# A mixer block on one core: weights and late x tiles moved to the second DMA ring, w1 loaded in three parts, and a new order of tiles

## The chip, the cores and the metric

The kernel runs on one core of a Trainium2 chip. TensorE does the matrix multiplications; DVE (VectorE), ScalarE and GpSimd do the other arithmetic; SyncE only issues transfers (DMAs). A "ring" is the queue of transfers that one engine, here SyncE or ScalarE, has issued. A transfer "lands" when the last of its data is reported. The "granted clock" is TensorE's clock as a share of full speed. The metric is the device time in microseconds, the median of several executions; the profile is of one execution. Its "span" (first to last instruction) is some 1.3 us shorter than the time. Ratios are the mean time of one kernel's fast runs over that of the other's of the same rounds, so not quite the ratio of the medians quoted.

## The reference

```python
B, S, D, F = 1, 2048, 512, 1792                      # bf16
h  = gelu(layernorm(x) @ w1)
hs = concat(h[:, :, 0:128]   shifted by +1 token, h[:, :, 128:256] by -1,
            h[:, :, 256:384] by +2,               h[:, :, 384:512] by -2) @ w2
x1 = x + hs
return x1 + gelu(layernorm(x1) @ w3) @ w4
```

2048 tokens are 16 tiles of 128. For each tile: statistics, norm, a transpose, the projection by w1 ("up1"), the mix by w2, a second norm and transpose ("tile 16 + t"), the up projection by w3 ("up2", in groups of tiles) and the down projection by w4.

## The kernel before

All instructions are recorded with their dependences and put in order by a list scheduler; what is tuned are the tables below. `SCRIPT` is TensorE's order. `ty:n` transposes tile n on TensorE (four matmuls against the identity and a copy by ScalarE or DVE); a tile without `ty` is transposed by a DMA issued from SyncE. `LOADS` is the order in which loads are issued; `@act` puts one on the ScalarE ring instead of SyncE's.

```python
GROUPS = {1: (1, 1, 1, 1, 2, 1, 4, 2, 2, 1), 2: (2, 4, 4, 2, 4)}
LOADS = """
x1 x2 tp2 x0@act w1a w1b x3 x4-5 tp5 w2a w2b x6-7 w3 tp17 w4a x8-10 w4b tp6 x11-12 tp1 tp16 x13-15
"""
SCRIPT = """
warm:9 sa:0 sb:0 ty:1 ra:0 rb:0 ty:2 up1:1 th:0 up1:2 mix:0 ty:3 ty:5 mix:1 ty:4 up1:3-4 ty:16 mix:2 ty:17
mix:3 up2:0 mix:4 up1:5 down:1 down:0 mix:5 up1:6-7 ...
"""
# ... the transpose of a tile that TensorE does not transpose
if q not in pe_tp:
    pg.add("sp", f"tp{q}",
           lambda e: e.dma_start(xT[:, :, P * t : P * (t + 1)], xn_buf[:, slot(q), :], transpose=True),
           reads=[(("xn", slot(q), hh), q) for hh in (0, 1)],
           writes=[(("xT", t, c), layer) for c in range(DC)], queue="tp")
# ... idle-filling matmuls at the start, on zeros
def f(e):
    for _ in range(n):
        ins = e.matmul(o_ps[:, b, :], zeros[:], rows, start=True, stop=True)
    return ins
```

In a load's name, w1a and w1b are halves of w1, `w1r` and `w1s` its last two quarters, x4-5 two tiles of x. The first tile runs as rows: `ra:0` and `rb:0` are two matmuls each over the first and second half of w1.

## Time and profile before

| | before |
|---|---|
| time | 135.79 us (135.78 to 136.6, 3 runs) |
| TensorE busy | 130.9 of 134.6 us, granted clock 1.00 |
| second row pair of tile 0 starts | 6.65 us |
| from there to the last matmul's end | 126.2 us |
| tile 6's DMA transpose | issued 15.96, landed 21.86, wanted 23.8 us |

The table is read from the chain of waits and from the records of the DMA engines, which give each packet's start and each landing. For what follows it matters that the first transpose by DMA is wanted only after all weights have landed (the last at 21.4 us). The lines stand in the prediction.

### The profile page before, as it was taken

The numbers are of one execution on the slowest core, as the hardware profiler recorded it, in microseconds if no ns is written. First come the engines' busy times: TensorE is split into PE (matmuls) and PEld (weight loads), VectorE is DVE, ScalarE is ACT, GpSimd is POOL, SyncE is SP. The second block draws the span as 40 slices with busy tenths as digits, with TensorE's granted clock in tenths as the row PEclk, the third lists the DMA queues.
The fourth block names the chain that finished last, engine by engine and source line by source line (L and its number), as shares of the span: only waits on it lengthen the run. The fifth ranks groups of instructions, "written<-read, shape, count | busy, mean of one in ns | idle before, by whom it ended". The sixth has DMA issues, their size and how long they took to land.

```text
span 134.6 us, 2001 instructions
## 1 busy us (share of the span) xinstructions
PE 130.9 (97%) x776; PEld 71.5 (53%) x789; DVE 50.8 (38%) x134; ACT 58.4 (43%) x92; POOL 29.7 (22%) x68
## 2 busy tenths in 40 slices
PE   8799999999999999999999999999999999999994
PEld 3287688544656444478544444444444444444464
DVE  2689996856178930070061004232222200012222
ACT  5779349989544275547315554000000155520000
POOL 2444549892102860006010001200000000000000
DMA  5999998445452134100411000211111100001112
GB/s 136 323 345 399 361 304 234 90 81 105 90 115 85 24 75 98 39 0 0 83 39 39 0 0 0 65 52 44 39 39 53 64 0 0 0 5 39 39 39 78
DMA packets 21289, 12.19 MB, mean 91 GB/s; under 512 B 13856, under 2 KB 20768, under 8 KB 21280
## 3 DMA queue, kind: packets, MB, share of 16 engines
q1 hardware_dynamic: 20704, 11.80, 32.7%
q10 hardware_dynamic: 576, 0.26, 0.7%
q8 instruction: 6, 0.10, 0.3%
q14 instruction: 3, 0.02, 0.1%
HBM read 6.82 MB, written 2.10 MB: 66 GB/s over the span
## 4 chain that ended last, share of the span: by engine, by line
PE 93%; DMA 4%; SPq 1%; issue 1%; DVE 0%
PE y_ps L626 46%; PE o_ps L695 36%; PE o_ps L666 10%; DMA w_sb<-in_w_dram 4%; PE y_ps L490 1%; SPq L368 1%; PE y_ps L528 0%; SPq L377 0%; DVE o_sb L703 0%; PE o_ps L594 0%; SPq L857 0%
## 5 line engine op out<-in xcount | busy, mean ns | idle before, releaser
L626 PE MATMUL y_ps<-xnT,w_sb 128*128 128x512 bf16 (+2 forms) x421 | 63.4, 308 | 0.2
L626 PEld LDWEIGHTS y_ps<-xnT,w_sb 128*128 128x128 bf16 x424 | 38.3, 98 | 24.8
L641 ACT ACTIVATE h2T<-y_ps 128x1024 bf16<-128x1024 f32 (+1 forms) x29 | 28.6, 993 | 48.8 <-PE y_ps L626 48.6
L695 PE MATMUL o_ps<-w_sb,h2T 128*128 128x512 bf16 (+3 forms) x247 | 48.6, 355 | 0.3
L695 PEld LDWEIGHTS o_ps<-w_sb,h2T 128*128 128x128 bf16 x252 | 23.5, 98 | 24.7
L703 DVE TENSOR_TENSOR o_sb<-o_ps,x_sb 128x512 bf16<-128x512 f32 (+3 forms) x18 | 11.4, 632 | 47.1 <-PE o_ps L695 47.1
L423 POOL TENSOR_TENSOR rstd<-mv,neghalf 128x1 f32<-128x1 f32 x21 | 11.5, 549 | 23.6 <-DVE mv L418 14.8
L416 DVE BATCH_NORM_STATS2 st<-x_sb 128x6 f32<-128x512 bf16 x21 | 14.1, 678 | 3.4 <-DMA x_sb<-in_x_dram 3.2
L666 PE MATMUL o_ps<-w_sb,hT 128*128 128x512 bf16 x59 | 14.9, 379 | 0.3
L423 POOL TENSOR_TENSOR rstd<-vpe,neghalf 128x1 f32<-128x1 f32 x11 | 6.0, 547 | 29.4 <-DVE vpe L412 29.3
L673 DVE SCALAR_TENSOR_TENSOR x_sb<-o_ps,x_sb 128x512 bf16<-128x512 f32 x5 | 3.4, 686 | 19.2 <-PE o_ps L666 19.2
L641 ACT ACTIVATE hT<-y_ps 128x512 bf16<-128x512 f32 (+1 forms) x10 | 8.1, 807 | 5.5 <-PE y_ps L626 5.3
L677 DVE TENSOR_TENSOR x_sb<-o_ps,x_sb 128x512 bf16<-128x512 f32 x11 | 7.6, 687 | 4.4 <-PE o_ps L666 4.1
L666 PEld LDWEIGHTS o_ps<-w_sb,hT 128*128 128x128 bf16 x64 | 6.0, 98 | 5.7
L457 POOL TENSOR_SCALAR xn_buf<-x_sb,rstd,nmr 128x512 bf16<-128x512 bf16 x11 | 8.4, 765 | 0.8 <-DVE nmr L450 0.4
L400 ACT ACTIVATE junk<-x_sb 128x512 bf16<-128x512 bf16 x11 | 6.9, 624 | 2.2 <-DVE x_sb L673 2.2
L454 ACT ACTIVATE xn_buf<-x_sb,nmr,rstd 128x512 bf16<-128x512 bf16 x8 | 6.3, 806 | 0.6 <-POOL nmr L450 0.6
L445 DVE TENSOR_SCALAR xn_buf<-x_sb,mv,rstd 128x512 bf16<-128x512 bf16 x12 | 5.3, 442 | 2.8 <-POOL rstd L423 2.6
L720 PE MATMUL o_ps<-zeros 128*128 128x512 bf16 x9 | 4.0, 631 | 0.4 <-DVE zeros L347 0.4
L395 ACT ACTIVATE junk<-x_sb 128x512 bf16<-128x512 bf16 x6 | 3.7, 624 | 0.8 <-DMA x_sb<-in_x_dram 0.8
L418 DVE BATCH_NORM_AGGREGATE mv<-st 128x2 f32<-128x9 f32 x21 | 3.8, 189 | 0.3
L450 POOL TENSOR_SCALAR nmr<-mv,rstd 128x1 f32<-128x1 f32 x13 | 3.4, 263 | 0.7
(34 smaller groups left out, 28.6 us busy)
## 6 DMA issues: line engine op xcount, KB each, us to landing
out_dram<-o_sb SPq DMA_DIRECT2D x15, 128.0 KB, 1.7
w_sb<-in_w_dram SPq DMA_DIRECT2D x1, 1792.0 KB, 9.7
w_sb<-in_w_dram SPq DMA_DIRECT2D x2, 896.0 KB, 11.5
w_sb<-in_w_dram SPq DMA_DIRECT2D x4, 256.0 KB, 5.2
x_sb<-in_x_dram SPq DMA_DIRECT2D x3, 256.0 KB, 5.1
x_sb<-in_x_dram SPq DMA_DIRECT2D x2, 384.0 KB, 8.9
x_sb<-in_x_dram SPq DMA_DIRECT2D x3, 128.0 KB, 2.6
xnT<-xn_buf SPq DMA_TRANSPOSE x24, 2.5
```

The lines of the kernel that those rows point to most:

```text
L400: (lambda d: (lambda e: e.activation(d, src, ACT_F.Square, accum_out=sums[:, q, 1:2])))(junk[:, b, :]),
L416: pg.add("dve", f"bnst{q}", lambda e: e.bn_stats(st9[:, q, 0:6], src), reads=rs, writes=[(("st", q), 0)], dur=605)
L423: lambda e: e.tensor_tensor(col(rstd), var, neghalf[:], ALU.pow),
L445: lambda e: e.tensor_scalar(dst, src, mv[:, q, 0:1], rstd[:, q : q + 1], ALU.subtract, ALU.mult),
L454: f = lambda e: e.activation(dst, src, ACT_F.Identity, bias=nmr[:, q : q + 1], scale=rstd[:, q : q + 1])
L457: f = lambda e: e.tensor_scalar(dst, src, rstd[:, q : q + 1], nmr[:, q : q + 1], ALU.mult, ALU.add)
L626: ins = e.matmul(y_ps[:, p, W * i : W * (i + 1)], wsb[:, dc, P * fc : P * (fc + 1)], src[:, dc, P * t0 : P * t0 + W], start=(dc == 0), sto ...
L641: (lambda d, s: (lambda e: e.activation(d, s, ACT_F.Gelu_apprx_tanh)))(dst, ysrc),
L666: ins = e.matmul(dst, hT[:, j, c0 : c0 + P], w2_sb[:, j, :], start=(j == 0), stop=(j == DC - 1))
L677: f = lambda e: e.tensor_tensor(x1_sb[:, t, :], dst, x_sb[:, t, :], ALU.add)
L695: ins = e.matmul(dst, h2T[:, fc, P * t : P * (t + 1)], w4_sb[:, fc, cs], start=(fc == 0), stop=(fc == FC - 1))
L703: (lambda d, c: (lambda e: e.tensor_tensor(o_sb[:, oi, c], d, x1_sb[:, t, c], ALU.add)))(dst, cs),
```

## The change

Intent: let SyncE's ring run dry early, so that its later DMA transposes do not stand behind loads; start w3, w4 and the late x tiles from ScalarE, after its first gelu; and with this earn a new order, with three transposes fewer on TensorE behind the first rows. `@act>name` means: on ScalarE's ring, in order behind the instruction `name`.

```diff
-GROUPS = {1: (1, 1, 1, 1, 2, 1, 4, 2, 2, 1), 2: (2, 4, 4, 2, 4)}
+GROUPS = {1: (1, 1, 1, 1, 1, 1, 1, 1, 1, 1, 2, 4), 2: (2, 4, 4, 2, 4)}
# ... the tables of which engine norms, copies and takes statistics of which tile change too
 LOADS = """
-x1 x2 tp2 x0@act w1a w1b x3 x4-5 tp5 w2a w2b x6-7 w3 tp17 w4a x8-10 w4b tp6 x11-12 tp1 tp16 x13-15
+x2 x3 x1 tp5 tp2 tp1 x0@act w1a w1s w1r x4 x5 w3@act>gelur0 tp5 x10-11@act>ev1act x14-15@act>gelu1_1_0 x6-7
+w4@act>ssq0 w2a tp4 x8 w2b x9 x13 x12
 """
 SCRIPT = """
-warm:9 sa:0 sb:0 ty:1 ra:0 rb:0 ty:2 up1:1 th:0 up1:2 mix:0 ty:3 ty:5 mix:1 ty:4 up1:3-4 ty:16 mix:2 ty:17
-mix:3 up2:0 mix:4 up1:5 down:1 down:0 mix:5 up1:6-7 ...
+warm:12 sa:0 sb:0 ty:2 ra:0 ty:3 rb:0 up1:2 ty:1 th:0 up1:3 ty:4 up1:1 up1:4 ty:5 mix:2 mix:0 up1:5 mix:1
+mix:3 up1:6 mix:4 up1:8 mix:5 up1:7 up1:9 mix:6-7 up2:0 mix:8 up1:10 down:1 mix:9 up1:11 ...
 """
```

More of the change, by code (lines that the diff above doesn't have):

```diff
@@ L31 @@
     LOOK = {"dve": 300.0, "act": 300.0}
-    DUE = 164483.0
+    DUE = 25310.8
     BEGIN = {"sp": 30.0, "act": 150.0, "pe": 400.0, "dve": 150.0, "pool": 450.0}
@@ L40, in __init__ @@
         self.lines = []
+        self.gates = []
     def add(self, eng, name, fn, reads=(), writes=(), dur=100.0, queue=None):
@@ L82, in order @@
                 order_only.add((named[a].idx, named[b].idx))
+        for a, b in self.gates:
+            assert named[a].eng == named[b].eng, (a, b)
+            order_only.add((named[a].idx, named[b].idx))
         last = None
@@ L161, in place @@
         fed = {}
-        clock = moved = last = self.total = 0.0
+        clock = moved = self.total = 0.0
+        last = {"sp": 0.0, "act": 0.0}
         out = []
@@ L198, in land @@
         def land(op):
-            nonlocal moved, last
+            nonlocal moved
             if op.queue == "tp":
-                at = max(clock + 500.0, op.start + 2450.0, last + 600.0) + self.LAG["tp"]
+                at = max(clock + 500.0, op.start + 2450.0, last[op.eng] + 600.0) + self.LAG["tp"]
             elif op.name.startswith("out"):
@@ L209, in land @@
             if op.queue != "tp":
-                last = max(last, at)
+                last[op.eng] = max(last[op.eng], at)
             op.landed = at
@@ L258, in place @@
         return out
-GROUPS = {1: (1, 1, 1, 1, 2, 1, 4, 2, 2, 1), 2: (2, 4, 4, 2, 4)}
-NORM = {0: "act", 3: "act", 7: "pool", 8: "act", 9: "pool", 10: "pool", 11: "pool", 12: "pool", 14: "act", 15: "act", 16: "pool", 18: "act", 19: "act", 24: "pool", 25: "act", 26: "pool", 27: "pool", 29: "pool", 30: "pool", 31: "act"}
-EVAC = {0: "both", 1: "both", 2: "both", 4: "both", 8: "both", 9: "dve", 10: "dve", 11: "dve", 12: "dve", 13: "dve", 14: "dve", 16: "dve", 17: "dve", 19: "both", 20: "both", 21: "both", 22: "both", 23: "both", 24: "dve", 25: "both", 27: "both", 29: "both", 30: "both", 31: "both"}
-STAT_ACT = (0, 7, 9, 12, 13, 15, 18, 21, 25, 29, 30)
+GROUPS = {1: (1, 1, 1, 1, 1, 1, 1, 1, 1, 1, 2, 4), 2: (2, 4, 4, 2, 4)}
+NORM = {2: "act", 5: "pool", 7: "pool", 9: "act", 10: "pool", 12: "pool", 13: "act", 14: "act", 18: "act", 20: "pool", 21: "pool", 24: "act", 25: "pool", 26: "act", 27: "pool", 28: "pool", 29: "pool", 30: "act", 31: "pool"}
+EVAC = {1: "both", 2: "dve", 3: "both", 4: "dve", 6: "dve", 11: "dve", 12: "both", 14: "both", 15: "both", 16: "dve", 17: "both", 18: "both", 21: "dve", 22: "both", 24: "both", 26: "both", 27: "dve", 28: "dve", 30: "dve"}
+STAT_ACT = (0, 17, 20, 21, 24, 27, 29, 31)
 TAIL = (256, 160, 96)
-NMR = {0: "pool", 1: "pool", 3: "pool", 5: "pool", 6: "pool", 7: "pool", 8: "pool", 9: "pool", 11: "pool", 13: "pool", 14: "pool", 15: "pool", 16: "pool", 17: "pool", 18: "pool", 20: "pool", 21: "pool", 22: "pool", 26: "pool", 27: "pool", 28: "pool", 29: "pool", 31: "pool"}
+NMR = {0: "pool", 5: "pool", 6: "pool", 7: "pool", 9: "pool", 10: "pool", 11: "pool", 14: "pool", 17: "pool", 18: "pool", 19: "pool", 24: "pool", 25: "pool", 29: "pool", 31: "pool"}
 NAT = (0,)
@@ L268 @@
 CSPLIT = ()
-HEV = {0: "dve", 4: "dve"}
-BIAS = {}
+HEV = {4: "dve", 5: "dve", 6: "dve"}
+BIAS = {"bnag1": -1094.39, "bnst1": -581.886, "bnst20": 900, "msq0": -779.351, "nmr5": -159, "norm4": 1237.6, "rstd25": 447, "sum3": -134.854, "tp6": 384, "tp8": 467, "vpe10": -1503, "vpe19": 6, "vpe2": 524}
 LOADS = """
-x1 x2 tp2 x0@act w1a w1b x3 x4-5 tp5 w2a w2b x6-7 w3 tp17 w4a x8-10 w4b tp6 x11-12 tp1 tp16 x13-15
+x2 x3 x1 tp5 tp2 tp1 x0@act w1a w1s w1r x4 x5 w3@act>gelur0 tp5 x10-11@act>ev1act x14-15@act>gelu1_1_0 x6-7
+w4@act>ssq0 w2a tp4 x8 w2b x9 x13 x12
 """
 SCRIPT = """
-warm:9 sa:0 sb:0 ty:1 ra:0 rb:0 ty:2 up1:1 th:0 up1:2 mix:0 ty:3 ty:5 mix:1 ty:4 up1:3-4 ty:16 mix:2 ty:17
-mix:3 up2:0 mix:4 up1:5 down:1 down:0 mix:5 up1:6-7 mix:8 mix:6 up1:9 mix:9-10 up1:8 mix:7 mix:11 up2:1
-mix:13 mix:15 up2:3 down:5 mix:12 up2:2 mix:14 down:2 down:4 down:3 down:6-8 down:11 down:9 up2:4 down:10
-down:12-15
+warm:12 sa:0 sb:0 ty:2 ra:0 ty:3 rb:0 up1:2 ty:1 th:0 up1:3 ty:4 up1:1 up1:4 ty:5 mix:2 mix:0 up1:5 mix:1
+mix:3 up1:6 mix:4 up1:8 mix:5 up1:7 up1:9 mix:6-7 up2:0 mix:8 up1:10 down:1 mix:9 up1:11 down:0 mix:10 up2:1
+mix:11 mix:15 up2:2 mix:12-13 up2:3 mix:14 down:2-3 down:7 down:6 down:4 up2:4 down:10 down:5 down:9 down:8
+down:11 down:14 down:13 down:12 down:15
 """
@@ L363, in load @@
             name, _, eng = item.partition("@")
-            eng = eng or "sp"
+            eng = eng.partition(">")[0] or "sp"
             if name[0] == "x":
@@ L744, in bass_standalone__mixer_s_mlp__prompt_kernel @@
                     op.first = i - 100
+                    if ">" in item:
+                        pg.gates.append((item.partition(">")[2], op.name))
                     queues[op.eng].append(op.name)
```

## The prediction

> **What bounds the kernel now.** I read the page's busy line and its slices first, then the chain of work that ended last in order of time, then the waits of TensorE, and last the timeline of the first 16 us with the issues of the DMA queue. The busy line and the slices, from the page:
>
> ```profile
> span 134.6 us, 2001 instructions
> PE 130.9 (97%) x776; PEld 71.5 (53%) x789; DVE 50.8 (38%) x134; ACT 58.4 (43%) x92; POOL 29.7 (22%) x68
> ...
> PE   8799999999999999999999999999999999999994
> ...
> DVE  2689996856178930070061004232222200012222
> ...
> DMA  5999998445452134100411000211111100001112
> ```
>
> TensorE is at 9 or more in every slice but the first two and the last; DVE and the DMA engines are full only in the slices from about 5 to 20 us. The chain (start, us, what):
>
> ```profile
> 1.47 5.13 DMA w_sb<-in_w_dram
> 6.61 0.05 issue
> 6.65 0.61 PE y_ps L528 x2
> 7.26 0.22 PE y_ps L490 x4
> 7.48 0.89 PE y_ps L626 x16
> ...
> 10.38 0.45 PE y_ps L490 x8
> ...
> 24.70 6.04 PE o_ps L695 x28
> ...
> 31.61 5.20 PE y_ps L626 x32
> ...
> 129.36 3.48 PE o_ps L695 x43
> 132.84 0.02 issue
> 132.87 0.26 DVE o_sb L703
> ```
>
> Up to 6.65 us the end is set by the second half of w1; from there to 132.84 us by TensorE alone. The waits of TensorE say the same; none is late:
>
> ```profile
> PE y_ps L528 <- DMA w_sb<-in_w_dram: 0.7, 1, 0.7
> PE o_ps L720 <- DVE zeros L347: 0.4, 1, 0.4
> ```
>
> So there are only two things to gain: an earlier 6.65, and fewer TensorE instructions after it. To check that nothing hides there I add the pieces up. A projection of one tile (16 matmuls, 128 wide) is 0.89, of two tiles 1.75, of four 5.20 - 1.75 = 3.45 (the 5.20 row is a four and a two); nine groups make 5 x 0.89 + 3 x 1.75 + 3.45 = 13.15. Sixteen mixes at 0.86: 13.8. The up projections: two groups of two at 6.1, three of four at 56 x 0.216 = 12.1: 48.5. The down projections 16 x 3.02 (half of 6.04): 48.3. Six transposes of four matmuls at 0.22 behind the rows, and the one of the gelu: 1.5. The two row matmuls: 0.6. Together 125.9, and 132.84 - 6.65 = 126.2. Stalls of before are 0.3 us in all; the change can't win there.
>
> [...] 0.89/16 = 55.6 ns, 6.04/28 = 215.7 ns. Regrouping tiles therefore changes little. [...] No second ring carries much before (0.26 MB), [...]. [...] The first x tile on the ScalarE ring agrees: its rows ran in one burst between 1.92 and 2.45 us while the rows of the other ring paused. [...] an issue is 0.4 to 0.5 us as a rule, but not behind much queued data:
>
> ```profile
> 3.99 0.47 SPq L368 DMA_DIRECT2D x_sb<-in_x_dram  x1
> 4.50 1.52 SPq L377 DMA_DIRECT2D w_sb<-in_w_dram  x2
> 6.07 3.59 SPq L368 DMA_DIRECT2D x_sb<-in_x_dram  x1
> 9.70 1.83 SPq L377 DMA_DIRECT2D w_sb<-in_w_dram  x1
> 15.96 2.20 SPq L463 DMA_TRANSPOSE xnT<-xn_buf  x1
> ```
>
> What follows w3 and half of w4 in the ring sat 3.59 us on SyncE. On SyncE that costs nothing; on ScalarE it would.
>
> **The change part by part.**
>
> *Start.* Before, SyncE issues x1, x2, then both halves of w1. After, it is x2, x3, x1, half, quarter, quarter. The last row of w1 is row 768 of the SyncE ring before and row 896 after. In the packet records row 768 starts at 4.75 us and the next 128 rows take 0.4 (row 896 at 5.16); but the third x tile also fills a pause between 2.6 and 2.9 us. The wait ended at 6.60, 1.85 us after that last row, because one of the 16 engines reported 1.3 us behind the other fifteen (5.30). I take the same lag. The start of the second row pair goes from 6.65 to about 6.95: +0.3 us. The quarters bring nothing by themselves, since both are needed at once.
>
> *Transposes.* Tiles 16 and 17 go from TensorE to the DMA (24 to 26 transposes there), and one more transpose lies ahead of the second row pair, in the time waited for w1 anyway. Six behind the rows become three: 3 x 0.22 = -0.67 us on the path. The three extra warming matmuls lie before 5.7 us even at the cold 0.43 each (9 end at 4.45), so also in that wait.
>
> *Groups.* Nine single tiles, one two, one four: 9 x 0.89 + 1.75 + 3.45 = 13.2 against 13.15: +0.06 us.
>
> *The rest of TensorE:* the same mixes, up and down projections, and the same tail of 256, 160 and 96 columns.
>
> *Loads.* w3, four late x tiles and w4 leave the SyncE ring. It is left with 2432 rows of 1 KB; from 5.0 us at 16 engines / 46 ns = 348 rows a microsecond they are through at about 9.5 us. w3 is issued behind the first gelu, near 8 us, and starts about 1.4 later: just when the other ring runs dry. At 140 ns for a row of 3.5 KB its 512 rows take 4.5 us, then 512 rows of x 1.5, then w4's 1792 rows 5.2: w3 by about 15, w4 by about 22 us. By the new order w3 is first used near 23 us and w4 near 32, so neither is waited for. Before, w3 landed at 14.2 for a use at 16.8 and w4 at 21.4 for 24.7.
>
> Sum on the path: +0.3 - 0.67 + 0.06 = -0.31 us, if no new wait appears.
>
> *The new waits.* The order is denser at the start: tiles 1 to 9 and eight mixes come ahead of the first up projection (before: four mixes), so DVE has less room. From 2.54 us I laid DVE's list out with its spacing in the trace (statistics 0.62 to 0.72, norm or full copy 0.34, residual 0.61): norm of tile 4 ends near 9.6 us and TensorE wants it at 9.7; tile 6 is normed near 12.4, behind the statistics of 8 and 7 and a GpSimd norm of 0.76. Its DMA transpose then lands at 12.4 + 2.5 = 14.9 alone. TensorE, at 6.95 + 0.5 (rows) + 5 x 0.89 (tiles 2, 3, 1, 4, 5) + 4 x 0.22 + 4 x 0.86 (mixes 2, 0, 1, 3) = 16.2, wants it then. The slack is 1.3 us, but w3 and x rows are in flight on the other ring: with a packet of eight w3 rows (8 x 0.14 = 1.1 us) ahead of some of its pieces it lands between 15.5 and 17.5. I count 0.1 us as the likely stall, with a tail to 1 or 2. ScalarE's issues cost 4 x 0.45 = 1.8 us of its sequencer between 8 and 12 us, where it has a few tenths of slack at each step.
>
> Prediction: 135.79 - 0.31 + 0.1 = 135.6 us.
>
> **The rivals.**
>
> *Late transposes.* Tiles 6, 8, 7 and 9 cross the ring of w3 and w4; at one row each in turn, tile 6's 32 pieces per engine would take 32 x (0.14 + 0.018) = 5 us during w3, and TensorE would stand 1 to 4 us at tile 6: 136.5 to 139. For it: before, transposes never met loads of another ring. Against: w3 is nearly through by then, and the burst of x0 shows packets of many rows, not single ones.
>
> *ScalarE or SyncE held at an issue.* If w4's 1792 rows hold ScalarE as the 3.59 us issue held SyncE, copy and gelu of tiles 4 and 5 wait, and TensorE some 2 us: about 138. [...] For it: the block is in the trace. Against: w4 is the last load on its ring, and the trace has the instruction after a large one held, not the large one itself.
>
> *A better start than I think.* If the engine that lags is ahead by the time of the later quarters, the start is 6.0 and the time 134.9.
>
> *DVE becomes the bound* between 8 and 16 us, with several stalls of 0.2 to 0.5 at copies and residuals: 136 to 136.8. For it: 9s in DVE's slices before; against: it had no TensorE wait in them.
>
> **Range and chances.** The sum without waits is 135.5, the better start 134.9, a stall of 1 to 2 us 136.5 to 137.5. So 135.0 to 137.2 eight times in ten. Faster by over 2% (under 133.1) would need 2.7 us where only 0.3 is stalls: 1 in 100. Slower by over 2% (over 138.5) needs one of the first two rivals in full: 7 in 100.
>
> **What would show it.** Right: the second row pair starts near 6.95; three transposes of 0.22 less on the chain; no wait of TensorE over 0.2 us after it; SyncE's transposes issued from about 12.5 us; w4 landed by about 22. Wrong: a gap in TensorE ahead of the projection of tile 6 (late transpose) or of tiles 4 and 5 (ScalarE held), a DMA issue over 1 us on ScalarE, a gap at 24 to 32 us for w3 or w4, or a start past 7.5.

## The result, and the profile after

The changed kernel takes 141.11 us (140.34 to 141.98, 4 runs) against 135.78: the ratio is 1.039 (95% interval 1.029 to 1.049). It is slower, and above the predicted range of 135.0 to 137.2. Two of its four runs have a mean granted clock of 0.976 and take 141.8 and 142.0; the two with a clock of 1.0 take 140.3 and 140.4. All count as fast. The profile is of a run of the first kind. From its page:

```profile
span 140.7 us, 2061 instructions
...
PE   8999639999999999999999999999999999999994
...
PEclk9999965899999999999999999999999999999999
```

One slice here is 3.5 us. TensorE has a hole in the fifth and sixth slice, and the granted clock falls in the sixth and seventh. The chain of waits, in order of time:

```profile
6.16 0.59 PE y_ps L535 x2
6.75 0.22 PE y_ps L497 x4
6.98 0.43 PE y_ps L535 x2
...
12.33 7.46 DMA xnT<-xn_buf
19.79 0.05 issue
19.84 1.89 PE y_ps L633 x16
21.73 1.71 PE o_ps L673 x4
23.43 1.71 PE y_ps L633 x16
25.14 1.14 PE o_ps L673 x4
26.28 1.79 PE y_ps L633 x32
```

Tile 6's transpose is issued at 12.33 us and lands 7.46 later; TensorE wanted it at 16.4. Behind it a projection of 16 matmuls takes 1.89 instead of 0.89 and a mix 1.71 instead of 0.86: half clock. By the trace's clock record it fell to half at 18.74 us, 2.3 us into the gap, and rose again at 25.57. The list of TensorE's waits has the wait itself:

```profile
PE y_ps L633 <- DMA xnT<-xn_buf: 3.4, 1, 3.4
```

and the busy times of three stretches (columns: stretch; its length and each engine's busy time; granted clock, DMA share, GB/s) show the clock and the busy DMA engines beside it:

```profile
12.40:16.30 3.90, 3.90 (x31) 2.10 (x29) 3.75 (x10) 2.03 (x4) 2.91 (x6) 1.00 0.99 355
16.30:19.84 3.54, 0.12 (x2) 0.01 (x1) 1.45 (x5) 0.79 (x3) 0.65 (x1) 0.84 1.17 292
19.84:26.00 6.16, 6.16 (x40) 4.49 (x41) 1.63 (x4) 1.42 (x3) 0.00 (x0) 0.54 1.19 278
```

The account of this run: the wait 3.42, and at half clock (1.89 - 0.89) + (1.71 - 0.86) + (1.71 - 0.89) + (1.14 - 0.86) = 2.95. Without both the span is 140.7 - 6.4 = 134.3, which is the predicted span without waits (134.6 - 0.31). So the whole miss lies between 16 and 26 us.

The transpose itself, from the records of the DMA engines: its 512 pieces of 256 bytes start at 16.32 us, 3.99 after the issue, and run until 19.03. Of transposes beside idle DMA engines (those issued from 29.5 to 41 us) the pieces start 1.2 us after the issue and take 0.75 to 0.84. The time is not lost at the issue: it held SyncE for 1.34 us, against 1.19 to 1.27 for those later ones, and SyncE's own loads had all started by 10.7 us.

### The profile page after: what moved, and what is told of

The parts are those of the page before. It is cut to its first block, busy times and chain, and to the rows that moved or that the text cites.

```text
span 140.7 us, 2061 instructions
## 1 busy us (share of the span) xinstructions
PE 134.7 (96%) x816; PEld 73.9 (53%) x816; DVE 51.0 (36%) x140; ACT 53.5 (38%) x76; POOL 29.4 (21%) x65
## 3 DMA queue, kind: packets, MB, share of 16 engines
q1 hardware_dynamic: 18976, 7.87, 23.5%
## 4 chain that ended last, share of the span: by engine, by line
PE 91%; DMA 5%; DVE 2%; issue 0%; ACT 0%; DVEq 0%
PE y_ps L633 43%; PE o_ps L702 34%; PE o_ps L673 8%; DMA xnT<-xn_buf 5%; PE o_ps L727 4%; DVE st L423 1%; PE y_ps L535 1%; PE y_ps L497 1%; DVE xnT L505 0%; ACT xnT L505 0%; DVE mv L425 0%; DVE xn_buf L452 0%; DVE o_sb L710 0%; PE o_ps L601 0%; DVE zeros L353 0%
## 5 line engine op out<-in xcount | busy, mean ns | idle before, releaser
L633 PE MATMUL y_ps<-xnT,w_sb 128*128 128x512 bf16 (+2 forms) x456 | 65.7, 305 | 3.4 <-DMA xnT<-xn_buf 3.4
L633 PEld LDWEIGHTS y_ps<-xnT,w_sb 128*128 128x128 bf16 x456 | 40.6, 101 | 28.9 <-DMA xnT<-xn_buf 3.9
L430 POOL TENSOR_TENSOR rstd<-mv,neghalf 128x1 f32<-128x1 f32 x24 | 13.3, 557 | 29.8 <-DVE mv L425 28.6
L423 DVE BATCH_NORM_STATS2 st<-x_sb 128x6 f32<-128x512 bf16 x24 | 16.1, 672 | 2.5 <-DMA x_sb<-in_x_dram 2.4
L673 PE MATMUL o_ps<-w_sb,hT 128*128 128x512 bf16 x64 | 16.8, 401 | 0.0
L684 DVE TENSOR_TENSOR x_sb<-o_ps,x_sb 128x512 bf16<-128x512 f32 x9 | 6.1, 685 | 15.1 <-PE o_ps L673 15.1
L430 POOL TENSOR_TENSOR rstd<-vpe,neghalf 128x1 f32<-128x1 f32 x8 | 4.6, 574 | 25.4 <-DVE vpe L419 25.4
L407 ACT ACTIVATE junk<-x_sb 128x512 bf16<-128x512 bf16 x8 | 5.0, 624 | 2.9 <-DVE x_sb L680 2.9
L727 PEld LDWEIGHTS o_ps<-zeros 128*128 128x128 bf16 x12 | 1.6, 144 | 3.2 <-issue 2.8
L457 DVE TENSOR_SCALAR nmr<-mv,rstd 128x1 f32<-128x1 f32 x9 | 1.9, 210 | 3.5 <-POOL rstd L430 3.4
```

The costliest lines, as they stand in the source:

```text
L423: pg.add("dve", f"bnst{q}", lambda e: e.bn_stats(st9[:, q, 0:6], src), reads=rs, writes=[(("st", q), 0)], dur=605)
L430: lambda e: e.tensor_tensor(col(rstd), var, neghalf[:], ALU.pow),
L633: ins = e.matmul(y_ps[:, p, W * i : W * (i + 1)], wsb[:, dc, P * fc : P * (fc + 1)], src[:, dc, P * t0 : P * t0 + W], start=(dc == 0), sto ...
L673: ins = e.matmul(dst, hT[:, j, c0 : c0 + P], w2_sb[:, j, :], start=(j == 0), stop=(j == DC - 1))
L684: f = lambda e: e.tensor_tensor(x1_sb[:, t, :], dst, x_sb[:, t, :], ALU.add)
```

## The experiments

Twelve kernels ran, all correct. In each, every engine's instructions are pinned to the order of the kernel it starts from, so that only the named edit differs. (A transpose moved to TensorE brings its copy with it, and leaves SyncE's list.) Before ran beside each (135.48 to 135.58). In the diffs, entries `tp..` of transposes are left out of `LOADS`; runs 1 and 8 take some of them out.

### 1. The old order with the loads moved

```diff
# tables and orders of before
-... w2a w2b x6-7 w3 w4a x8-10 w4b x11-12 x13-15
+... w2a w2b x6-7 x8-10 x11-12 w3@act>gelur0 x13-15@act>gelu1_1_0 w4@act>ssq0
```

> The old order, tiles and engines of before with every instruction pinned; only w3, tiles 13 to 15 and w4 go to the ScalarE ring behind the first gelu (tiles 8 to 12 stay on SyncE). Theory (the harm is that the new order needs tile 6's DMA transpose at 16 us, while loads are in flight; here it is needed at 23.8): no wait of TensorE, 135.4 to 136.2 us. Rival (the ScalarE ring itself costs: issues hold ScalarE, or its rows hold up SyncE's loads): over 137 us with waits before 20 us.

Measured: 136.05 us, ratio 1.0053 (1.0035 to 1.0071). The list of TensorE's waits:

```profile
PE y_ps L632 <- DMA xnT<-xn_buf: 0.2, 1, 0.2
```

Moving the loads alone costs half a per cent and no stall beyond this: here, too, tile 6's transpose was slow (issued at 15.43, first piece at 19.76), but it is wanted at 23.3. The harm needs the new order, which wants it 7 us earlier.

### 2 and 3. w4 later, or half of it later

```diff
-w4@act>ssq0
+w4@act>gelu1_9_0                                   # run 2
+w4a@act>ssq0 ... w4b@act>gelu1_9_0                 # run 3
```

> The changed kernel, every order pinned, w4's issue moved from 11.4 us to behind the gelu of tile 9 (near 21 us). Theory A ([...] SyncE's transpose queues behind them): first packet of tile 6's transpose near 13.6 us in place of 16.3, landing 16.5 to 17.5, TensorE waits 0.5 to 1.3 us, no half clock, 136 to 137 us. Theory B (the rows of w3 and x on the DMA engines starve it): first packet stays near 16, landing near 18.3, wait 2 us, 137 to 138 us.

> The changed kernel, orders pinned, w4 in two halves: 896 rows at 11.4 us as before, the other 896 behind the gelu of tile 9. Theory A: [...] tile 6's transpose has its first packet near 13.6 us and TensorE waits about 1 us: 136 to 137.5 us. Theory B: as in the changed kernel, first packet near 16.3, landing near 19.7, wait 3.4 us, 140 to 142 us.

Measured: 143.98 us (1.062) and 142.24 us (1.050). In run 2 the first piece of tile 6's transpose starts at 15.68, 3.60 us after its issue, with no w4 issued at all; in run 3 at 16.32, 4.08 after. Theory A, that SyncE's transpose queues behind w4's 1792 rows, falls: w4 isn't needed for the delay. Theory B was nearer on the first piece, but long rows aren't needed either, as run 1 showed with rows of 1 KB only (4.33 us). Its time for run 2, 137 to 138 us, was missed by 6. Run 2 is even slower than the changed kernel because the late w4 met the transposes of tiles 11 and 10 (issued 29.17, first piece 33.45); two waits, 4.6 us in all. Moving a load moved the collision.

### 4. Keeping TensorE busy in the gap

```diff
-mix:3 up1:6 mix:4
+mix:3 warm:15 up1:6 mix:4
```

> The changed kernel with 15 idle-filling matmuls of 512 columns (3.2 us) ahead of the projection of tile 6, to keep the granted clock at full. If the half clock after the gap costs its full 2.9 us: 138.2 us. If it hides behind later transposes (tiles 8, 7 and 9 landed at 21.8, 24.7 and 26.2 in the changed kernel, so a TensorE at full clock waits for them): new waits of 0.3, 1 and 0.5 us at those tiles and 139.8 to 140.5 us, as in the two runs of the changed kernel whose clock was 1.0.

Measured: 140.81 us (1.042), clock 1.0 in every run. TensorE's timeline (start, length, in brackets the idle time before and what ended it):

```profile
15.89 3.41 PE L727 MATMUL o_ps<-zeros 128*128 128x512 bf16 x15
19.74 1.07 PE L633 MATMUL y_ps<-xnT,w_sb 128*128 128x128 bf16 x16 [0.45 <-DMA xnT<-xn_buf]
...
21.77 1.07 PE L633 MATMUL y_ps<-xnT,w_sb 128*128 128x128 bf16 x16
...
24.72 1.07 PE L633 MATMUL y_ps<-xnT,w_sb 128*128 128x128 bf16 x16 [1.02 <-DMA xnT<-xn_buf]
25.96 1.07 PE L633 MATMUL y_ps<-xnT,w_sb 128*128 128x128 bf16 x16 [0.18 <-DMA xnT<-xn_buf]
```

The second branch held in kind, 0.3 us above its range and with the waits spread otherwise. With the clock up, TensorE reaches tiles 7 and 9 early and waits for their transposes instead. The end is set by the last of this train: tile 9's projection starts at 25.96, where by the sum of the work it could have started near 21. So the half clock and the later waits overlap, and the clock is worth not its 2.95 us but the 1.5 us by which the runs of the changed kernel differ.

### 5. Nothing in flight beside the transpose

```diff
-w3@act>gelur0
+w3@act>gelu1_6_0        # tiles 10, 11, 14, 15 and w4 follow it in the ring
```

> The changed kernel, orders pinned, w3 and what follows it on the ScalarE ring held back to behind the gelu of tile 6 (near 17 us), so that nothing else is in flight when tile 6's transpose is issued at 12.3 us. Theory (a DMA transpose is slow only beside loads in flight, of either ring): first packet 1.2 us after the issue, landing near 14.9 us, no wait of TensorE at tile 6; the cost moves to a wait for w3 (landing near 24 to 25) and to the transposes behind it, 137 to 140 us. Rival (the transpose is slow by its own place in the SyncE queue): landing near 19.5 as in the changed kernel.

Measured: 142.86 us (1.052). Tile 6's transpose, issued at 12.74, has its first piece at 13.99 (1.25 us) and its last at 14.74, and lands at 15.29. TensorE runs through tiles 6, 8 and 7 without a wait; tile 9 is the last line:

```profile
16.65 1.06 PE L633 MATMUL y_ps<-xnT,w_sb 128*128 128x128 bf16 x16
...
18.41 1.06 PE L633 MATMUL y_ps<-xnT,w_sb 128*128 128x128 bf16 x16
...
20.17 1.06 PE L633 MATMUL y_ps<-xnT,w_sb 128*128 128x128 bf16 x16
23.54 1.54 PE L633 MATMUL y_ps<-xnT,w_sb 128*128 128x128 bf16 x16 [2.31 <-DMA xnT<-xn_buf]
```

Tile 9's transpose was issued at 17.10, and w3 at 17.75, right behind it. Its pieces ran in time, from 18.27 to 19.02, but the 4-byte packets that report it ran only from 21.43 to 23.17, among w3's rows, and it landed at 23.49. So loads in flight can hold up the report of a transpose whose data has already moved. The total is worse than expected, as the late loads cost more than I gave them: these 2.3 us, and DVE waited 7.0 us for a late x tile. But the question is settled: the same transpose from the same place in SyncE's queue is fast when no loads are in flight. The profile's page also shows the granted clock falling behind this gap (seventh and eighth slice), though it is shorter than that of the changed kernel:

```profile
PE   8979993699988999999999999999999999999994
...
PEclk9999998699999999999999999999999999999999
```

### 6. Tile 6 alone on TensorE

```diff
-up1:5 mix:1 mix:3 up1:6 mix:4
+up1:5 ty:6 mix:1 mix:3 up1:6 mix:4
```

> The changed kernel with tile 6 alone transposed on TensorE (0.22 us more there), the rest pinned. Theory (a queue of late transposes): tile 8's is now first of the queue and lands near 19.8 us where TensorE wants it at 18.2, tile 7 and 9 follow near 21.8 and 24; the wait moves to tiles 8, 7 and 9, in all some 3 us: 138 to 139.5 us, clock 1.0. Rival (tile 6's wait and the half clock after it are all the loss): 135.5 to 136 us.

Measured: 143.01 us (1.054), clock 0.988 in its fast runs. The rival is out, but so are my numbers: I expected 138 to 139.5 at a clock of 1.0. Its profile fell in the slow state (145.18 us at a clock of 0.976, the fast runs 142.89 to 143.1), so I use it only for the pattern: three waits for transposes, the train having merely moved to tiles 8, 7 and 9. Why it is slower than the changed kernel isn't settled.

### 7. Tiles 6 and 8 on TensorE, w4 behind tile 9

```diff
-up1:5 mix:1 mix:3 up1:6 mix:4 up1:8
+up1:5 ty:6 mix:1 mix:3 up1:6 ty:8 mix:4 up1:8
-w4@act>ssq0
+w4@act>gelu1_9_0
```

> The changed kernel with tiles 6 and 8 transposed on TensorE and w4 issued behind the gelu of tile 9. Transposes of tiles 7 and 9 then cross only w3 and x: tile 7 lands near 18.5 for a use at 20.1, tile 9 near 20.5 for 21.0. Theory: at most 0.5 us of waits, 135.6 to 136.4 us, level with before. If w4 in flight from 23 us delays the transposes of tiles 10 and 11 past 31 us, up to 138.

Measured: 136.99 us (1.011). The waits at tiles 6 to 9 are gone and the clock is 1.0; of the 5.3 us, 4.1 are recovered. What is left is the wait that I had named as the risk, at tiles 10 and 11, whose transposes meet w4 (issued 23.70, first piece 27.86):

```profile
PE y_ps L633 <- DMA xnT<-xn_buf: 1.1, 1, 1.1
```

### 8. All loads on one ring, new order

```diff
-... x4 x5 w3@act>gelur0 x10-11@act>ev1act x14-15@act>gelu1_1_0 x6-7 w4@act>ssq0 w2a x8 w2b x9 x13 x12
+... x4 x5 x6-7 w2a x8 w2b x9 w3 x10-11 w4 x13 x12 x14-15
```

> The changed kernel with its new order pinned, but all loads on the SyncE ring as in before (w3, tiles 10 and 11, w4 behind tile 9, then tiles 12 to 15), transposes behind them. Theory (the new order needs the transpose too early for any placing of the loads): tile 6's transpose waits for the whole ring and lands at 21 us or later, TensorE waits 5 us or more: 143 to 147 us, worse than the changed kernel. Rival (the second ring causes the loss): below 138 us.

Measured: 146.0 us (1.076), with one wait of 7.7 us at tile 6, whose first piece starts at 21.33. So the second ring helps the new order; it doesn't help enough.

### 9. w3 in four transfers

```diff
-w3@act>gelur0
+w3p@act>gelur0 w3q@act>gelur0 w3r@act>gelu1_2_0 w3s@act>ev1act
```

> The changed kernel, orders pinned, w3 on the ScalarE ring in four transfers of 128 rows (8 rows of 0.14 us per DMA engine each) instead of one of 512. Theory C (the DMA engines turn to the other ring only between transfers): first packet of tile 6's transpose within 1.1 us of its usual 1.2, by 14.8 us; landing 16.5 to 18, wait at tile 6 of 0.5 to 1.5 us, the train of tiles 8, 7, 9 still late, 138.5 to 140.5 us. Theory D (the delay of 4 us beside a saturated ring does not depend on the cut): first packet 16 to 16.3, as in the changed kernel, 140 to 142 us.

Measured: 142.05 us (1.048). First piece at 16.65, 3.95 us after the issue. Theory C, that the engines turn to the other ring only between transfers, falls; cutting w3 in four made no difference.

### 10 to 12. Repairs

```diff
# 10: run 7 and
-warm:12
+warm:9
# 11: run 10 and
-w4@act>gelu1_9_0
+w4@act>ssq20
# 12: run 10 and
-up2:0 mix:8 up1:10
+up2:0 ty:10 ty:11 mix:8 up1:10
```

> The repaired kernel of the seventh run (tiles 6 and 8 on TensorE, w4 behind the gelu of tile 9) with 9 warming matmuls instead of 12. Theory (the last three warming matmuls, at half clock 0.43 us each, delay the first transposes): the first row pair starts near 5.7 us in place of 6.2, 136.5 us against 137.0. Rival (w1 or the norms set the start): 137.0 and the same start.

> As the tenth run, with w4 issued 1.5 to 2 us earlier, behind the second gelu after tile 6's (tile 8), so that w4's rows are through by 27.5 us when the transposes of tiles 11 and 10 come. Theory: the wait of 1.1 us at tile 10 and 11 goes, tiles 16 and 17 still cross before w4's rows start; 135.3 to 135.8 us, level with before. Rival: w4 now meets the transposes of tiles 16 and 17 and TensorE waits before the first up projection, 136 to 138 us.

> As the tenth run (tiles 6 and 8 on TensorE, w4 behind the gelu of tile 9, 9 warming matmuls), with tiles 10 and 11 transposed on TensorE too, so that no transpose that is wanted soon crosses loads. Theory (crossing loads is the only loss left; each transpose moved costs 0.22 us): the wait of 1.3 us goes, 0.45 comes, 137.3 - 0.85 = 136.4 us, no wait of TensorE over 0.3 us from 7 us on; still behind before, since the order's whole saving in transposes is then given back. Rival (DVE or another bound): 137 us or more with waits elsewhere.

Run 10: 137.29 us (1.013), level with run 7 within the intervals. In its profiled execution the first row pair starts at 5.64 instead of 6.21, as expected, and the wait at tiles 10 and 11 is 1.3 instead of 1.1; that execution is 0.5 us shorter than run 7's (136.95 against 137.45), but the medians are not. The start differs between executions, too: in the eight fast profiles with 12 warming matmuls the first row pair starts anywhere from 5.5 to 6.5 us, the earlier the earlier the clock rose (at 3.5 us in run 5, at 6.2 in run 9), and in the three with 9 at 5.6 to 5.7. So the earlier start is likely, and a gain in time isn't shown.

Run 11: 140.37 us (1.034), one of six executions slow. The rival held, and cost more than its 136 to 138: w4, issued at 19.46, was 0.15 us ahead of the transpose of tile 17 (19.61), whose first piece then came at 23.56; in run 10, with w4 behind it, the same transpose started after 1.27 us. TensorE waits 3.1 us before the first up projection.

Run 12: 136.99 us (1.0105). No wait for a transpose is left, but another takes its place, for DVE's copy of a transposed tile:

```profile
PE y_ps L633 <- DVE xnT L505: 0.4, 1, 0.4
```

0.6 short of what I expected. The chain that leads to this wait runs on DVE and GpSimd from 20.1 to 31.7 us. Run 12 also has seven transposes behind the rows where before has six, 0.22 us more. These two are the parts that I can name of the 1.45 us to before. No version tried beats before.

### The delay of a transpose, collected

From the packet records: time from issue to first piece, and what the ScalarE ring moved, per DMA engine, between 1.2 us after the issue and that piece.

| transpose | first piece after, us | other ring meanwhile, per engine |
|---|---|---|
| tile 6, run 5 | 1.25 | nothing |
| tile 17, run 10 | 1.27 | nothing |
| tile 7, run 7 | 1.33 | the ring's last 20 rows or so in flight |
| tile 6, changed kernel | 3.99 | 64 KB (13 rows of w3, 19 of 1 KB) |
| tile 6, run 2 | 3.60 | 55 KB |
| tile 6, run 4 | 3.97 | 64 KB |
| tile 6, run 9 (w3 in four) | 3.95 | 58 KB |
| tile 6, run 1 | 4.33 | 67 KB, all rows of 1 KB |
| tile 11, run 7 | 4.16 | 62 KB, all rows of 1 KB |
| tile 17, run 11 | 3.94 | 43 KB, all rows of 1 KB |

So a transpose that meets a well-filled other ring has its first piece 3.6 to 4.3 us after the issue in place of 1.2, whether the rows are of 1 KB alone or mixed with w3's of 3.5 KB, and with w3 cut in four as well; 43 to 67 KB per engine go first. Afterwards the two rings go nearly one row to one piece (in the changed kernel 40 rows for the 32 pieces of each engine), which makes 2.7 us of 0.75. Whether a number of bytes, a time or something else sets the delay is not shown. Run 11 speaks against a fixed number of bytes: its DMA engines moved 258 GB/s in that time, those of the changed kernel 380, and the delay is the same.

## Why the prediction was wrong, point by point

- **The step that failed** is "The new waits": "with a packet of eight w3 rows (8 x 0.14 = 1.1 us) ahead of some of its pieces it lands between 15.5 and 17.5. I count 0.1 us as the likely stall". It landed at 19.79 and TensorE waited 3.42 us. Issue (12.33 against 12.4) and want (16.4 against 16.2) were right; the duration of the transfer was mis-sized: 7.46 us, not 3 to 5. The packet of eight rows was an estimate, from one burst of 8 rows per DMA engine at the start of the trace (1.92 to 2.45 us) to the turn-taking of two full rings, and no transpose beside another ring's loads was in the trace.
- **The rival "Late transposes"** is what happened, with a wait at tile 6 inside its 1 to 4 us, but by another course: its one row to one piece came, for 2.7 us, only after some 4 us without a piece. And its 136.5 to 139 was too low on two counts. Tiles 8, 7 and 9 were late too (landed at 21.84, 24.71 and 26.23, in a train), and I had counted tile 6 alone; run 4 shows the train. And I left out the clock: in the profiled run the gap was 3.42 us and the clock fell to half 2.3 us into it; two of four runs kept it (mean granted clock 1.0), and what decides between them is not shown. In run 5 it fell behind a gap of 2.31 us, in run 11 behind one of 3.13 us (the 56 matmuls after it took 7.87 us instead of 6.11).
- **"Start"** was right in number (6.98 against 6.95) by luck, as the reason was wrong. No DMA engine lagged behind w1 this time: its last quarter landed at 5.99. In the profiled execution the 12 warming matmuls set it: they ended at 5.48, and the transposes for the first rows wait for them. Other executions of the same start differ (see run 10).
- **"Transposes", "Groups", "The rest"**: right. The span less the wait and the half clock is 134.3, as summed (with the start right by luck).
- **"Loads"**: right that nobody waits for w3 and w4, though w3 landed at 17.1 (said: 15) and w4 at 26.2 (said: 22). SyncE's loads ran until 10.7 us, not 9.5, beside w3's first rows; w4's rows shared the DMA engines with the transposes.
- **The rival "ScalarE or SyncE held at an issue"** fell: ScalarE's four issues took 0.38 to 0.61 us, and runs 2 and 3 clear w4.
- **The rival "DVE becomes the bound"** did not show in the changed kernel, but a wait of 0.4 us for DVE does in run 12, once the late transposes are out of the way.
- **Chances**: slower got 7 in 100, because I believed the collision short without a measurement of one.

## What to carry to other kernels

Don't issue a transfer that is wanted soon while another ring is full: here a second ring gave it no lane of its own (3.6 to 4.3 us to the first piece). Do the small one on an engine, which recovered 4.1 of 5.3 us in run 7, or issue the bulk after it has landed and not just behind its issue, as tile 9 in run 5 shows. When an order is made denser, check the first use of everything that crosses the DMA engines at that time, and look at the last of a train of transfers, not at the first. A duration taken from a quiet part of a trace isn't valid in a busy one: a transpose took 2.5 us to landing as the median of each of the two kernels, and 7.46 for tile 6 beside loads.
